# Three small moves in the schedule of an attention and GLU kernel: a late weight's buffers, the gates' exponentials and additions, and the routing's steps

## The chip, the cores and the metric

The kernel runs on one core of a Trainium2 chip. The core has five engines that work side by side and meet only at semaphores: TensorE (PE in the profile; PEld is its loading of weights), VectorE (DVE), ScalarE (ACT), GpSimd (POOL) and SyncE (SP), which issues the DMAs. The metric is the device time of one launch in microseconds (us), the median of several runs. Before the change it is 1688.54 us, from three runs of 1688.06 to 1691.13.

## What is computed

One input `x` of 2048 tokens by 512 features goes through two branches, and a gate per token mixes them. All data are float32.

```python
x = A_x
g = _sigmoid((x * gate_w).sum(-1, keepdims=True))     # routing: one number per token
# branch A: attention, 32 heads of 16 features, softmax over all 2048 keys, then wo
scores = jnp.einsum("bhqd,bhkd->bhqk", q, k) * scale
p = _softmax(scores, axis=-1)
o = jnp.einsum("bhqk,bhkd->bhqd", p, v)
a = o.transpose(0, 2, 1, 3).reshape(B, S, D) @ wo
# branch B: gated linear unit with 1792 inner features
h = _sigmoid(x @ w_gate) * (x @ w_up)
b = h @ w_down
return g * a + (1 - g) * b
```

## The kernel before

**Arithmetic.** Most products are made from operands split into a high and a low part (`split`, L99; `terms`, L142): three matmuls, high by high, high by low and low by high, stand for one float32 product. A split is a copy on one engine (high) and a subtraction on another (low), and a matmul that takes the low part waits for both.

**Stages.** First the queries and keys of the first heads, and the values, are made. Then come 256 periods (`for k in range(NPER)`, L889). A period k treats two of the 16 blocks of 128 keys for one pair of heads and one half of the queries (L668): it makes eight tiles of scores, which ACT turns into exponentials (`st_part`, L681), and then the value products (`values`, L821, matmuls of L829), which add up exponentials times values and, in a 17th row, the softmax's denominators. The sums of eight periods are collected by POOL (L846) and stored to `pv_d`. In each period up to k = 244 there also run eight tiles of scores for a later pair, of which DVE takes the maximum (`sm_step`, L292 to L294). When the 64 tiles of a half are done (`count`, L296), which is at k % 8 == 4, DVE makes the half's maxima out of them and transposes them (L298, L300), and POOL splits them. In the gaps of the row groups TensorE computes everything else in `dense` halves (L162): the remaining queries and keys, the gates and ups of the GLU, and the first heads' share of `wo`. A closing stage (from L945) then runs over 28 chunks (`for n, (c, f) in enumerate(chunks)`, L1009): it multiplies pairs of hidden feature blocks with `w_down` (L1019), with the remaining part of `wo` in between (L149), and stores the output.

**What sets the order.** The order on TensorE, ACT, DVE and POOL is that in which the code issues the instructions. Within a period it is written out by hand in a string, one for periods with maxima and one for the last eleven (`FREE` is 245, `NPER` 256):

```python
STEADY = ("m1:3 t0:2 m0:4 d1 d1 t0:5 m0:6 d1 d1 t0:1 d1 m0:3 d1 t0:2 turn m0:0 t1:4 "
          "m1:5 d0 d0 t1:1 t1:6 d0 m1:2 d0 m1:3 d0 t1:4 d0")
LAST = "t0 d1 t0 d1 t0 d1 turn t0 t1 t1 d0 t1 d0 t1 d0"
```

`m` is a tile of maxima, `t` a tile of scores with its exponential, `d` a half of the dense work, and the number a PSUM bank. A bank is free for the next tile when DVE or ACT has read it. POOL's work waits in lists with an estimated cost for each step and is issued in portions (`work`, L182). Only SP's queue, which issues nearly all DMAs in order, is put in order by the framework's planner from its own estimates.

**The places of the change.**
- *Routing.* `logits` (L814) is DVE's product of 128 tokens with `gate_w`, with a sum. The loop calls it for two blocks of tokens in each group of six periods from k = 75 to 122, at r = 3 and r = 4 of the group (L902). The tokens lie in a tile with the tag `ev`, of which there are two buffers.
- *Denominators.* `denominators` (L781) is a generator: a load, reciprocals on DVE (L787), a store. The loop takes one step of the first chain of them after the value products in each of the periods 192 to 211 (L928). What POOL multiplies with the heads later comes from `rec_d`, which it stores.
- *Early hidden chunks.* The first two chunks of the GLU's hidden layer are made inside the last periods (`hidden_early`, L749). Their gates and ups are loaded at k = 239. Their eight exponentials run on ACT, two in each of the periods 242 to 245, ahead of the value products (L919). The rest are 32 small DVE steps: additions of one (`tensor_scalar`, L759), reciprocals (L763), products (L766), and the split into `xh` and `xl` (L770, L772). The loop takes one of them after the value products of k = 243 and 244 and three after those of each later period. From k = 245 on DVE also empties the value products' bank (L836) and the bank of the dense work (through `leave`, an operation listed under L469), which ACT does before.
- *Late weights.* The rows of `w_down` from the third block on are loaded and split late (`down_late`, L723, called by `late_next`, L950, once before the closing stage and once after each chunk). ACT makes the high parts and POOL the low ones. Weights 2 and 3 go to buffers of the tags `wh` and `wl`, weights 4 and 5 to those of `sum` and `part`, which hold the value products' sums and the last addend before that, and the others to tiles of their own. The two buffers of the tag `wr` hold raw weights; the last of these, `wd0r` and `wd1r`, are split by POOL at k = 241 and 242. A raw late weight lies in an `ev` buffer, which comes free when POOL has made the low parts.

Of the kernel before, what the change touches and what calls it, by code (L numbers as in the profile page):

```python
# [37 lines left out]
NPER = NSTEP // 2  # L38
FREE = NPER - LEAD // 2
# [7 lines left out]
def gated_mix(ctx, tc, x, xT, wqk, wv, wo, w_gate, w_up, w_down, gate_w, out):  # L47
# [51 lines left out]
    def split(h, l, src, hi, lo):  # L99
        if hi is act:  # L100
            act.activation(h, src, AF.Copy)  # L101
        else:
            hi.tensor_copy(h, src)
        return lo.tensor_tensor(l, src, h.bitcast(F32), ALU.subtract)  # L104
# [66 lines left out]
    def turn(*runs):  # L171

        token = pool.nop()
        tc.add_manual_dep(token.ins, runs[-1].last.ins.name, SYNC, reason=SHARED)
        for r in runs:
            r.token = token
# [5 lines left out]
    def work(length):  # L182
        length -= over[0]
        while length > 0.3 and (later or turnover or slow):
            cost, step = (later or turnover or slow).pop(0)
            step()
            length -= cost
        over[0] = max(0.0, -length)
# [52 lines left out]
    def load_pair(p, cols=slice(0, S)):  # L241
        for t, src in enumerate((q_d, k_d)):
            for b in range(2):
                rows, r = slice((2 * p + b) * DH, (2 * p + b + 1) * DH), 64 * b
                to = (QS, KS)[t][p % 2]
                if t == 0:
                    two, one = src[:, rows, cols].rearrange("a d s -> d a s"), src[0, rows, cols]
                else:
                    two, one = src[0, rows, cols].unsqueeze(1), src[1, rows, cols]
                    two = two.to_broadcast([DH, 2, cols.stop - cols.start])  # L250
                sp.dma_start(to[r:r + 2 * DH, cols].bitcast(F32), two)
                sp.dma_start(to[r + 2 * DH:r + KM, cols].bitcast(F32), one)
# [50 lines left out]
    def put_max(half):  # L303

        p, i = half
        mt = mrow.pop(half)
        hl = keep.tile([P, 2, 32], F32R, name=f"mhl{p}_{i}", tag="mhl", bufs=2)

        def low():
            pool.tensor_tensor(hl[:, 1, :], mt, hl[:, 0, :].bitcast(F32), ALU.subtract)  # L310
            d = max_d[2 * p + i]
            sp.dma_start(d.rearrange("k r a j -> (k r) a j"), hl.bitcast(F32))
            for b in (1, 0):
                for a in range(2):
                    r = 64 * b + 3 * DH + a
                    rows_in[p, i] = sp.dma_start(QS[p % 2][r:r + 1, i * 1024:(i + 1) * 1024].rearrange(
                        "o (t k j) -> o t k j", t=8, k=4).bitcast(F32),
                        d[:, 8 * b:8 * b + 8, a, :].rearrange("k t j -> t k j").unsqueeze(0))
        return [(1.6, lambda: pool.tensor_copy(hl[:, 0, :], mt)), (0.25, low)]  # L319
# [348 lines left out]
    def st_part(k, b):  # L668

        p, r = divmod(2 * k, 32)  # L670
        i, kt = divmod(r, 16)
        qs, ks = QS[p % 2], KS[p % 2]
        r = 64 * b
        pt = ptile[k, b] = mid(f"p{k}_{b}")
        for a in range(2):
            for c in range(2):
                o = bank()
                q0 = i * 1024 + c * 512
                pe.matmul(o, ks[r:r + KR, (kt + a) * P:(kt + a + 1) * P], qs[r:r + KR, q0:q0 + 512],  # L679
                          start=True, stop=True)  # L680
                act.activation(pt[:, 2 * a + c, :], o, AF.Exp, scale=DH ** -0.5)  # L681
                yield
# [29 lines left out]
    def hidden_load(c, f):  # L712
        gu = big(f"gul{c}_{f}").rearrange("p (a f s) -> p a f s", a=2, f=2)
        for a in range(2):
            sp.dma_start(gu[:, a], gu_d[a, f:f + 2, :, c * 512:(c + 1) * 512].rearrange("f p s -> p f s"))
        return gu

    def late_raw(src, r):
        raw = keep.tile([P, 2, D], F32, name=f"late{r}", tag="ev", bufs=2)
        sp.dma_start(raw, src[r * P:(r + 2) * P, :].rearrange("(k p) d -> p k d", p=P))  # L720
        return raw

    def down_late(f, raw):  # L723
        if f < 6:
            th, tl, bufs = ("wh", "wl", 4) if f < 4 else ("sum", "part", 2)
            for a in range(2):
                h = keep.tile([P, D], F32R, name=f"wd{f + a}h", tag=th, bufs=bufs)
                l = keep.tile([P, D], F32R, name=f"wd{f + a}l", tag=tl, bufs=bufs)
                split(h, l, raw[:, a, :], act, pool)
                wd.append((h, l))  # L730
        else:
            fs = slice(f - 6, f - 4)
            split(wd_h[:, fs, :], wd_l[:, fs, :], raw, act, pool)
            wd.extend((wd_h[:, f - 6 + a, :], wd_l[:, f - 6 + a, :]) for a in range(2))
# [58 lines left out]
    def split_load(r):  # L793
        f, t, c = r // 8, r // 4 % 2, r % 4
        e = split_in[r] = keep.tile([P, 2, 512], F32R, name=f"sq{r}", tag="ev", bufs=2)
        sp.dma_start(e[:, 0, :].bitcast(F32), s_d[t, f, :, c * 512:(c + 1) * 512])

    def split_sum(r):
        f, t, c = r // 8, r // 4 % 2, r % 4
        e = split_in.pop(r)  # L800

        def store():
            for a in range(2):
                sp.dma_start((q_d, k_d)[t][a, (2 + f) * P:(3 + f) * P, c * 512:(c + 1) * 512],
                             e[:, 1 - a, :].bitcast(F32))
        split_later(e[:, 1, :], e[:, 0, :], e[:, 0, :].bitcast(F32), store)
# [3 lines left out]
    def logit_load(t):  # L810
        tok[t] = keep.tile([P, 2, D], F32, name=f"xn{t}", tag="ev", bufs=2)
        sp.dma_start(tok[t], x[t * P:(t + 2) * P, :].rearrange("(t p) d -> p t d", p=P))

    def logits(t, a):  # L814
        xn = tok[t][:, a, :]
        dve.tensor_tensor_reduce(xn, xn, gwb, scale=1.0, scalar=0.0, op0=ALU.mult, op1=ALU.add,
                                 accum_out=logit[:, t + a:t + a + 1])
# [50 lines left out]
    def emit(order, **parts):  # L868

        for word in order.split():  # L870
            if word == "turn":
                if run:
                    turn(run)
                work(2.0)
            else:
                kind, _, b = word.partition(":")
                spot[:] = [seven[int(b)]] if b else []
                next(parts[kind], None)
# [10 lines left out]
    for k in range(NPER):  # L889
        n = 2 * k  # L890
        if n + LEAD == NSTEP:
            bank = bank7
            leave = dve.tensor_copy
        if 75 <= k < 123:
            t, r = divmod(k - 75, 6)
            if r in (0, 3):
                split_load(2 * t + r // 3)
            if r in (1, 4):
                split_sum(2 * t + r // 3)
            if r == 1:  # L900
                logit_load(2 * t)
            if r in (3, 4):  # L902
                logits(2 * t, r - 3)
        if n % 32 == 0 and n // 32 + 1 < NPAIR:
            load_pair(n // 32 + 1)
        parts["t0"], parts["t1"] = st_part(k, 0), st_part(k + 1, 1) if k + 1 < NPER else iter(())
        emit(STEADY if k < FREE else LAST, **parts)
        if run and run.done():
            run = next(fill, None)
        elif run and run.n:  # L910
            turn(run)
        for half in list(mrow):
            later[:0] = put_max(half)
        work(2.6)
        later.extend(soon)
        soon.clear()
        if k == NPER - 1:
            break
        if NPER - 15 < k <= NPER - 11:  # L919
            for _ in range(2):  # L920
                next(next(exps))
        spot[:] = [seven[SUMS]]
        values(k)
        if k == NPER - 17:
            loaded.extend(hidden_load(*chunks[m]) for m in range(2))
            early = [hidden_early(m) for m in range(2)]
            exps = iter([early[0]] * 4 + [early[1]] * 4)
        if 192 <= k < 212:  # L928
            next(dens[0], None)
        if k == NPER - 6:  # L930
            next(dens[1])
        if k == NPER - 2:
            raws = [late_raw(*late[m][:2]) for m in range(2)]
        if k == NPER - 13:
            early = chain(*early)
        if k >= NPER - 13:
            for _ in range(1 if k < FREE else 3):
                next(early, None)

    flush(later)  # L940
# [133 lines left out]
```

## Time and profile before

The profile shows one execution of 1689.49 us. Its instructions span 1687.7 us; the rest lies before the first and after the last. TensorE was granted its full clock (1.000). The table gives the stages of that execution: bounds from the span's start, and busy time of each engine in us.

| stage | from | to | PE | DVE | ACT | POOL |
|---|---|---|---|---|---|---|
| first products, until the value products of k = 1 | 0 | 96.18 | 94.12 | 81.69 | 36.27 | 12.55 |
| periods with maxima, k = 2 to 244 | 96.18 | 1454.46 | 1358.11 | 1216.32 | 1214.78 | 869.17 |
| last periods, k = 245 to 255 | 1454.46 | 1497.06 | 42.44 | 33.23 | 42.60 | 15.43 |
| closing stage | 1497.06 | 1687.70 | 185.34 | 121.04 | 69.10 | 39.41 |

TensorE's matmuls overlap one another, so that its busy share is near 100% everywhere and says little. More telling is how far apart two like places of the schedule lie: the first matmul of the value products of one period and that of the next.

A row of the timeline reads: start in us, duration, engine, line of the kernel, operation, output and inputs by the program's names, shapes, count. What stands in brackets is the idle time of the engine just before and what ended it. A count over one means that rows close together were merged; the duration is then that of the group. A row of stages ("windows") reads: bounds, length, then busy time of PE, PEld, DVE, ACT and POOL with counts, the granted clock, the DMA engines' busy share and GB/s.

### The profile page before, as it was taken

Reading aid. Unit: us, or ns where it says so; the run is one execution under the profiler, and the core shown is the slowest. Engines: PE = TensorE matmul, PEld = TensorE weight load, DVE = VectorE, ACT = ScalarE, POOL = GpSimd, SP = SyncE. Lnnn points to the kernel's source line nnn. Section 1 sums busy time; section 2 is a strip of 40 time slices with the busy share of each in tenths; the row PEclk is TensorE's granted clock in tenths of the full one; section 3 lists DMA queues with packets and bytes.
Section 4 is the critical chain, followed back from the end, with each engine's and each line's share of the span. In section 5 each row is a group of like instructions: output and inputs, shape, how many; then the busy total and the mean of one; then the engine's idle time right before and its main releaser. Section 6 shows DMA issues by size and latency. Waiting matters only on the chain.

```text
span 1687.7 us, 34644 instructions
## 1 busy us (share of the span) xinstructions
PE 1680.0 (100%) x12485; PEld 1026.4 (61%) x12485; DVE 1452.3 (86%) x2347; ACT 1362.8 (81%) x2657; POOL 936.6 (55%) x920
## 2 busy tenths in 40 slices
PE   9999999999999999999999999999999999999999
PEld 7755555555555555555555555555555555558887
DVE  7988888888889999999888888889998888787753
ACT  4188898988988898889898898989888888984331
POOL 1034476647656666566676766666666667543110
PEclk9999999999999999999999999999999999999999
DMA  7511447366555554555635353534343435358862
GB/s 237 148 46 59 127 175 210 133 165 207 149 194 137 163 153 153 162 162 187 158 102 146 102 145 107 139 102 135 102 129 114 133 113 169 106 184 282 299 216 71
DMA packets 143756, 254.20 MB, mean 151 GB/s; under 512 B 24224, under 2 KB 36512, under 8 KB 140704
## 3 DMA queue, kind: packets, MB, share of 16 engines
q1 hardware_dynamic: 135968, 237.30, 46.2%
q10 hardware_dynamic: 7616, 14.68, 2.7%
q8 instruction: 98, 1.61, 0.4%
q14 instruction: 74, 0.61, 0.1%
HBM read 149.42 MB, written 102.50 MB: 149 GB/s over the span
## 4 chain that ended last, share of the span: by engine, by line
PE 97%; issue 1%; DVE 1%; POOL 0%; DMA 0%; ACT 0%; SPq 0%; POOLq 0%; DVEq 0%
PE dn L162 30%; PE sm L829 27%; PE sm L292 13%; PE st L679 7%; PE sm L1019 5%; PE sm L679 4%; PE st L292 2%; PE dn L1019 2%; PE st L162 2%; PE st L1019 2%; PE st L643 1%; PE st L149 1%; PE sm L149 1%; PE st L829 0%; DVE stat L294 0%
## 5 line engine op out<-in xcount | busy, mean ns | idle before, releaser
L294 DVE TENSOR_REDUCE stat<-sm 128x1 f32<-128x512 f32 x1313 | 849.4, 682 | 142.1 <-PE sm L679 129.3
L681 ACT ACTIVATE p<-st 128x512 f32<-128x512 f32 x1019 | 619.4, 655 | 1.1 <-PE st L679 0.6
L681 ACT ACTIVATE p<-sm 128x512 f32<-128x512 f32 x1027 | 611.6, 633 | 0.8 <-PE sm L679 0.5
L292 PE MATMUL sm<-ks,qs 48*128 48x512 f32 x1313 | 516.3, 435 | 0.2
L294 DVE TENSOR_REDUCE stat<-st 128x1 f32<-128x512 f32 x735 | 479.9, 681 | 0.1
L829 PE MATMUL sm<-p,v 128*17 128x512 f32 x4016 | 480.0, 595 | 0.0
L679 PE MATMUL sm<-qs,ks 64*128 64x512 f32 x1027 | 427.3, 419 | 0.0
L679 PE MATMUL st<-qs,ks 64*128 64x512 f32 x1019 | 426.1, 419 | 0.2 <-ACT p L681 0.2
L292 PEld LDWEIGHTS sm<-ks,qs 48*128 48x128 f32 x1313 | 234.0, 184 | 291.7 <-DVE stat L294 211.5
L846 POOL TENSOR_TENSOR sum<-sum,part 128x512 f32<-128x512 f32 x224 | 288.6, 1288 | 136.0 <-PE sm L679 119.0
L292 PE MATMUL st<-ks,qs 48*128 48x512 f32 x735 | 290.4, 395 | 0.0
L829 PEld LDWEIGHTS sm<-p,v 128*17 128x17 f32 x4016 | 93.1, 96 | 225.9 <-issue 155.1
L834 ACT ACTIVATE part<-sm 128x512 f32<-128x512 f32 x214 | 128.1, 599 | 126.5 <-issue 86.0
L542 POOL TENSOR_TENSOR chain<-chain,chain 128x512 f32<-128x512 f32 x96 | 124.0, 1292 | 156.8 <-PE sm L679 143.1
L679 PEld LDWEIGHTS st<-qs,ks 64*128 64x128 f32 x1019 | 187.5, 184 | 29.9 <-issue 3.4
L679 PEld LDWEIGHTS sm<-qs,ks 64*128 64x128 f32 x1027 | 189.4, 185 | 9.9 <-issue 5.1
L542 POOL TENSOR_TENSOR had<-chain,had 128x512 f32<-128x512 f32 x96 | 123.5, 1286 | 40.1 <-PE sm L679 17.1
L292 PEld LDWEIGHTS st<-ks,qs 48*128 48x128 f32 x735 | 137.1, 187 | 1.4 <-ACT v L662 0.3
L607 ACT ACTIVATE chain<-dn 128x512 f32<-128x512 f32 x128 | 89.1, 696 | 0.0
L542 POOL TENSOR_TENSOR side<-side,side 128x512 f32<-128x512 f32 x32 | 41.3, 1291 | 78.6 <-PE sm L679 74.1
L104 POOL TENSOR_TENSOR ol<-ot,oh 128x512 fp32r<-128x512 f32 (+1 forms) x8 | 15.0, 1871 | 98.2 <-ACT oh L101 84.4
L319 POOL CAST mhl<-mt 128x32 fp32r<-128x32 f32 x32 | 7.5, 236 | 104.1 <-DVE mt L300 104.1
(913 smaller groups left out, 3223.7 us busy)
## 6 DMA issues: line engine op xcount, KB each, us to landing
gul<-gu_d SPq DMA_DIRECT2D x56, 512.0 KB
had<-gu_d SPq DMA_DIRECT2D x84, 256.0 KB
gu_d<-had SPq DMA_DIRECT2D x84, 256.0 KB
gu_d<-side SPq DMA_DIRECT2D x56, 256.0 KB
pv_d<-sum SPq DMA_DIRECT2D x32, 256.0 KB
qs<-q_d SPq DMA_DIRECT2D x30, 256.0 KB
ks<-k_d SPq DMA_DIRECT2D x30, 256.0 KB
gu_d<-far SPq DMA_DIRECT2D x28, 256.0 KB
```

The costliest lines, as they stand in the source:

```text
L149: pe.matmul(o, a, b, start=(i == 0), stop=(i == len(ops) - 1))
L162: mm = pe.matmul(self.o, a[rows], b[rows], start=(self.n == 0), stop=(self.n == 2 * len(self.ops) - 1))
L292: pe.matmul(t, qs[r:r + KM, qt * P:(qt + 1) * P], ks[r:r + KM, g * 512:(g + 1) * 512], start=True, stop=True)
L294: dve.tensor_reduce(stat[half][:, b, qt % 8, g:g + 1], t, axis=AX.X, op=ALU.max)
L542: pool.tensor_tensor(to, u, w, ALU.add)
L607: leave = lambda e, o: act.activation(e, o, AF.Copy)
L679: pe.matmul(o, ks[r:r + KR, (kt + a) * P:(kt + a + 1) * P], qs[r:r + KR, q0:q0 + 512], start=True, stop=True)
L681: act.activation(pt[:, 2 * a + c, :], o, AF.Exp, scale=DH ** -0.5)
L829: pe.matmul(o[32 * c:32 * c + VW, :], v[:, 2 * k % 16 + a, h * VW:(h + 1) * VW], pts[c // 2][:, 2 * a + c % 2, :], start=(a == 0), stop=(a ...
L834: act.activation(e, o, AF.Copy)
L846: pool.tensor_tensor(s, s, e, ALU.add)
L1019: pe.matmul(down[t], a, b, start=(f == 0 and m == 0), stop=(f == NF - 2 and m == 5))
```

## The change

Four edits, all in the order of the work or in the choice of buffers; no operation is added or removed.

1. The last of the weights that were put into `sum` and `part`, number 5, goes into the two `wr` buffers, its high part in the one and its low part in the other.
2. The second `logits` of a group moves from r = 4 to r = 5 in the groups that begin at k % 8 == 1, which are those at 81 and 105: it moves from k = 85 to 86 and from 109 to 110.
3. The steps of the first chain of denominators skip the periods with k % 8 == 4 and run to k = 214 instead of 211, the same twenty steps.
4. The exponentials of the early hidden chunks begin at k = 241 instead of 242 and end at 244. The DVE steps behind them begin at k = 242 instead of 243; from 245 on a period takes two of them if k is odd and four if it is even, instead of three.

```diff
         if f < 6:
             th, tl, bufs = ("wh", "wl", 4) if f < 4 else ("sum", "part", 2)
             for a in range(2):
+                if f + a == 5:
+                    th = tl = "wr"
                 h = keep.tile([P, D], F32R, name=f"wd{f + a}h", tag=th, bufs=bufs)
                 l = keep.tile([P, D], F32R, name=f"wd{f + a}l", tag=tl, bufs=bufs)
                 split(h, l, raw[:, a, :], act, pool)
...
-            if r in (3, 4):
-                logits(2 * t, r - 3)
+            if r == 3:
+                logits(2 * t, 0)
+            if r == (5 if (k - r) % 8 == 1 else 4):
+                logits(2 * t, 1)
...
-        if NPER - 15 < k <= NPER - 11:
+        if NPER - 16 < k <= NPER - 12:
             for _ in range(2):
                 next(next(exps))
...
-        if 192 <= k < 212:
+        if 192 <= k < 215 and k % 8 != 4:
             next(dens[0], None)
...
-        if k == NPER - 13:
+        if k == NPER - 14:
             early = chain(*early)
-        if k >= NPER - 13:
-            for _ in range(1 if k < FREE else 3):
+        if k >= NPER - 14:
+            for _ in range(1 if k < FREE else 2 if k % 2 else 4):
                 next(early, None)
```

## The prediction

> **What bounds the kernel now.** I read the page first, then the stretch of each period, then DVE, ACT and POOL where a period is too long.
>
> ```profile
> span 1687.7 us, 34644 instructions
> PE 97%; issue 1%; DVE 1%; POOL 0%; DMA 0%; ACT 0%; SPq 0%; POOLq 0%; DVEq 0%
> ```
>
> The chain that ends last is PE for 97% of the span, so an edit gains only where PE stands still, or where the other engines stretch its order. I cut the span at the first value product (L829) of each period; a window from one such start to the next is one period's length.
>
> ```profile
> 554.31:559.89 5.58, 5.58 (x47) 3.23 (x45) 5.48 (x11) 5.00 (x11) 1.61 (x2) 1.00 0.55 139
> 559.89:565.75 5.86, 5.86 (x46) 3.17 (x45) 5.79 (x13) 5.20 (x11) 3.50 (x5) 1.00 0.41 130
> 694.43:700.31 5.88, 5.88 (x46) 3.11 (x44) 5.81 (x13) 5.22 (x11) 3.50 (x5) 1.00 0.41 133
> 1185.99:1191.70 5.71, 5.71 (x46) 3.12 (x44) 5.57 (x12) 5.13 (x11) 2.90 (x5) 1.00 0.18 63
> 1230.76:1236.82 6.06, 5.95 (x46) 3.12 (x44) 5.86 (x12) 5.21 (x11) 2.94 (x5) 1.00 0.18 60
> 1426.56:1454.46 27.90, 27.90 (x222) 16.17 (x220) 24.70 (x42) 26.18 (x55) 22.11 (x20) 1.00 0.57 193
> 1454.46:1458.29 3.83, 3.83 (x32) 1.75 (x30) 2.42 (x6) 3.83 (x9) 1.37 (x3) 1.00 0.20 73
> 1458.29:1494.08 35.79, 35.63 (x272) 16.25 (x271) 27.83 (x39) 35.79 (x75) 13.32 (x12) 1.00 0.24 78
> ```
>
> The first column after the bounds is the length, then come the busy times of PE, PEld, DVE, ACT and POOL. A period with maxima lasts 5.58 (first row; the sixth is five of them, 27.90). Rows two to five are the periods that end with the value products of k = 85, 109, 197 and 205: too long by 0.28, 0.30, 0.13 and 0.48. All four follow a period in which a half's maxima are completed (k % 8 == 4). A last period takes 3.83 at best, but the nine of the eighth row take 35.79 where nine at 3.83 are 34.47: 1.32 too much, with ACT busy throughout.
>
> **Denominators.** Their reciprocals leave k = 196, 204 and 212; the loop runs three periods longer.
>
> ```profile
> 1233.05 0.54 DVE L787 RECIPROCAL den<-den 32x64 f32<-32x64 f32 x1
> 1233.62 0.69 DVE L294 TENSOR_REDUCE stat<-sm 128x1 f32<-128x512 f32 x1
> ```
>
> An undisturbed period's first reduce starts 2.38 after the value products before it (568.13 below, less 565.75). Here it starts 2.86 after 1230.76, which is 0.48 late, exactly the period's excess: PE needs the bank that this reduce frees. Without the reciprocal it could start in time. The reciprocals at other k cost nothing now: DVE has 0.70 idle there (below), more than 0.54. **Term: 0.13 + 0.48 = 0.61 gained.** Load and store of the denominators stay one call from their reciprocals, in the same order on SP.
>
> **Logits.** The second of two goes from k = 85 to 86 and from 109 to 110.
>
> ```profile
> 562.56 0.68 DVE L294 TENSOR_REDUCE stat<-sm 128x1 f32<-128x512 f32 x1
> ```
>
> ```profile
> 566.15 1.27 DVE L294 TENSOR_REDUCE stat<-sm 128x1 f32<-128x512 f32 x2
> 568.13 0.69 DVE L294 TENSOR_REDUCE stat<-sm 128x1 f32<-128x512 f32 x1 [0.70 <-PE sm L679]
> ```
>
> At k = 85 the reduce starts 2.67 after 559.89, late by 0.29, and the period is 0.28 long. Taking the logit away gains 0.28, and 0.30 at 109. But at k = 86 it must fit between 567.35 and 568.13, and POOL is there:
>
> ```profile
> 567.16 0.73 POOL L448 TENSOR_TENSOR side_9r<-side_9r 128x256 f32<-128x256 f32 x1
> ```
>
> The first logit of all met the same POOL operation:
>
> ```profile
> 521.98 1.28 DVE L816 CUSTOM_DVE_ANT_0 xn<-xn,gwb 128x512 f32<-128x512 f32 x1
> ```
>
> ```profile
> 521.98 0.73 POOL L448 TENSOR_TENSOR side_8r<-side_8r 128x256 f32<-128x256 f32 x1
> ```
>
> It took 1.28 and ended 0.55 after POOL's end: it ran only then. At k = 86, with DVE and POOL both 0.28 earlier, POOL works from 566.88 to 567.61 and the logit asks at 567.07; it ends at 568.16, and the reduce due at 567.85 starts at about 568.1: 0.25 late. The like at k = 110. Bounds of one giveback: 0 (DVE comes first) and 0.30 (all of it). I take 0.25, the row at 521.98 being this very pair. **Term: 0.58 - 0.51 = 0.07 gained.**
>
> **Gates' exponentials and additions.** The exponentials go from k = 242..245 to 241..244; there ACT has 27.90 - 26.18 = 1.72 idle in five periods, of which two carry a pair already: 0.57 in each of the other three, and a pair takes 0.80. As the five are no longer for those two pairs (5 x 5.58), I cost the pair at 241 at nothing; without that cover it costs the 0.23 by which it is too long. It reads loads that SP issues from the end of k = 239 on; no row here gives their landing, and if they are late, ACT and all behind it wait. The first addition now comes at k = 242, behind its last reduces:
>
> ```profile
> 1443.70 1.28 DVE L294 TENSOR_REDUCE stat<-sm 128x1 f32<-128x512 f32 x2
> 1445.68 0.69 DVE L294 TENSOR_REDUCE stat<-sm 128x1 f32<-128x512 f32 x1 [0.70 <-PE sm L679]
> ```
>
> ```profile
> 1444.81 1.29 POOL L136 TENSOR_TENSOR wd1l<-wd1r,wd1h 128x512 fp32r<-128x512 f32 x1
> ```
>
> ```profile
> 1450.47 0.41 DVE L759 TENSOR_SCALAR gul<-gul 128x512 f32<-128x512 f32 x1
> ```
>
> The addition takes 0.41 and the gap is 0.70. But it would ask at about 1444.9, and POOL's subtraction began at 1444.81 and ends at 1446.10. If it must wait as the logit did, it ends near 1446.4 and the reduce due at 1445.68 is 0.65 late, with PE behind it. Bounds: 0 and 0.65; I take **0.65 lost**, since POOL is first by 0.08. [...] No row of this trace shows a 512-wide addition behind a POOL operation.
>
> **The last periods.** Here ACT has no slack, and the pair that leaves k = 245 costs it directly:
>
> ```profile
> 1460.80 0.80 ACT L755 ACTIVATE gul<-gul 128x256 f32<-128x256 f32 x2
> ```
>
> That is 0.61 to 0.80 of the 1.32 too much. Most of the rest is DVE's: every second period it also empties the heads' bank, behind three operations of the gates.
>
> ```profile
> 1479.68 0.68 DVE L469 COPY hp<-dn 128x512 f32<-128x512 f32 x1
> ```
>
> ```profile
> 1480.26 0.50 PE L679 MATMUL st<-qs,ks 64*128 64x512 f32 x1
> 1480.50 0.47 PE L162 MATMUL dn<-wo0h,xh 64*128 64x512 f32 x1
> ```
>
> The copy ends at 1480.36, and PE's dn product starts 0.24 behind the product that it should run beside. Two operations at odd k and four at even k leave the copy its time.
>
> ```profile
> L763 DVE RECIPROCAL gul<-gul 128x128 f32<-128x128 f32 x16 | 13.8, 913 | 0.0
> ```
>
> Two periods then hold at most six of these, two value copies and one heads' copy: 6 x 0.913 + 3 x 0.68 = 7.5 of 7.66. Bounds: 0.5 (only the pair's time, part of it hidden) and 1.32 (all). **Term: 1.1 gained**, nearer the upper end, as the pair and the late copies are both named in the rows.
>
> **The late weight.** wd5 now takes the buffers of wd0r and wd1r, last read by POOL at 1446.10, so its split waits for no store.
>
> ```profile
> 1510.43 0.39 PE L1019 MATMUL dn<-wd4l,hl 128*128 128x512 f32 x1
> 1510.66 0.39 PE L1019 MATMUL dn<-wd4h,hl 128*128 128x512 f32 x1
> 1511.57 0.50 PE L1019 MATMUL dn<-wd5h,hl 128*128 128x512 f32 x1 [0.52 <-ACT wd5h L101]
> 1512.93 0.50 PE L1019 MATMUL dn<-wd5l,hl 128*128 128x512 f32 x1 [0.85 <-POOL wd5l L104]
> 1513.27 0.39 PE L1019 MATMUL dn<-wd5h,hl 128*128 128x512 f32 x1
> ```
>
> ```profile
> 1510.89 0.63 ACT L101 ACTIVATE wd5h<-late 128x512 fp32r<-128x512 f32 x1 [5.05 <-DMA pv_d<-sum]
> ```
>
> From 1510.66 on, three steps take 2.61 instead of 3 x 0.23 (the step before them), 0.69: 1.92 lost. ACT's wait of 5.05 goes entirely: wd5h starts at 1505.84. What is late next?
>
> ```profile
> 1506.21 1.28 POOL L104 TENSOR_TENSOR wd4l<-late,wd4h 128x512 fp32r<-128x512 f32 x1
> 1511.59 1.28 POOL L104 TENSOR_TENSOR wd5l<-late,wd5h 128x512 fp32r<-128x512 f32 x1 [4.11 <-ACT wd5h L101]
> ```
>
> ```profile
> 1506.38 2.19 DVE L747 TENSOR_TENSOR gul<-gul 128x1024 f32<-128x1024 f32 x1 [0.25 <-DMA gul<-gu_d]
> 1508.49 1.21 DVE L104 TENSOR_TENSOR hl<-gul,hl 128x1024 fp32r<-128x1024 f32 x1
> ```
>
> DVE's product already waits for POOL's wd4l (2.19, not 1.21). POOL's wd5l now stands behind it and would run from 1508.5 to 1509.75, as in this pair, where POOL asked first and DVE's low part waited:
>
> ```profile
> 1518.27 2.43 POOL L104 TENSOR_TENSOR wd_l<-late,wd_h 128x1024 fp32r<-128x1024 f32 x1 [0.91 <-ACT wd_h L101]
> ```
>
> ```profile
> 1518.36 3.42 DVE L104 TENSOR_TENSOR hl<-gul,hl 128x1024 fp32r<-128x1024 f32 x1
> ```
>
> The low part of hl then ends near 1510.9, where PE wants it at 1510.66: 0.25 lost. Later, PE already meets a low part just as it ends:
>
> ```profile
> PEld sm L1019 <- DVE hl L104: 0.2, 1, 0.2
> ```
>
> It hangs on loads that SP issues behind the late weights' low parts. These move up by most of the 1.92, not all; I take 0.2 more. Bounds: 0 (the loads do not move) and 1.92. **Term: 1.45 gained**, nearer the upper end, since ACT, which splits the late weights, is free 5 us sooner. SP's order is the planner's; I take it as it is now.
>
> **Sum:** 0.61 + 0.07 - 0.65 + 1.1 + 1.45 = 2.6. The profiled run took 1689.49 (span 1687.7 and 1.8 around it) and becomes 1686.9; the median, 0.95 below it, 1688.54, becomes **1685.9**.
>
> **Rivals.**
> *The covers hold* (30%): the logits and the addition get DVE's port first, and the closing stage keeps more: 0.58 + 0.61 + 1.2 + 1.6 = 4.0, 1684.5. For it: POOL leads by only 0.08 to 0.2. Against: two rows of blocking.
> *The loads are the bound of the closing stage* (16%): PE, 1.92 sooner, waits that much more for the low part of hl. The tail's term is 0, the rest 1.13: 1687.4. For it speaks the wait just shown; against, that the late raws are asked for sooner.
> *DVE becomes the bound of the last periods* (12%): at even k it has four operations and two copies, 4 x 0.913 + 2 x 0.68 = 5.0 in 3.83. If the bank of the value products (seven take turns) is needed before odd k's slack repays this, PE waits 1.2 in each of five periods: 6 lost, 1688.54 - 2.6 + 6 = 1692, slower. It decides from 0.5 a period (2.6 in all). Against: each period's copies stand ahead of its own operations, and the two periods together still fit (7.5 of 7.66).
> That the weight would still wait is excluded: nothing reads the new buffers after 1446.10.
>
> **Numbers.** 0.2% (3.4 us) is about what a measurement can tell from no change. My forecast, 42%, reaches from 1685.0 to 1686.8, nearly all within it (34 points; 8 faster). The covers' rival is faster for 27 of its 30 points, the loads' rival is the same, DVE's slower for 7 of 12. So faster 0.35, same 0.58, slower 0.07. The range takes in the first three: the covers' sum with 0.6 of scatter, 1683.9, to the loads' with 0.3, 1687.7.
>
> **What would show it.** Periods 85, 109, 197 and 205 back at 5.58; 86 and 110 at about 5.83 with a logit over 1 us long; the period that ends with the value products of k = 243 at 6.2 with an addition over 1 us; nine last periods near 34.7; no ACT wait for pv_d, and wd4 to wd5 without a gap. I am wrong if these additions and logits stay at 0.41 and 0.68, if a low part of hl stops PE for over 1 us behind 1511, or if DVE's copies run late at odd k.

## The result, and the profile after

The changed kernel takes 1692.5 us, the median of 14 runs (1690.93 to 1694.6), against 1688.56 for the kernel before (14 runs, 1687.62 to 1691.13). The ratio is 1.0022 with a 95% interval of 1.0014 to 1.0030: slower by 3.9 us, where I had forecast 2.6 less. The profiled execution took 1693.09, with a span of 1691.3. Its chain of work that ended last:

```profile
PE 95%; DVE 2%; DMA 2%; issue 0%; POOL 0%; SPq 0%; ACT 0%; DVEq 0%; POOLq 0%; ACTq 0%
```

PE's share fell from 97% to 95%, and DMA and DVE have 2% each: in some stretch of the chain something other than TensorE now decides. To find where, I cut both spans at two marks of the schedule, the first value product of k = 1 and that of k = 255. The two stretches behind the first mark, before:

```profile
1500.05:1687.70 187.65, 182.35 (x809) 148.78 (x808) 118.52 (x108) 66.13 (x72) 37.87 (x19) 1.00 0.67 222
96.18:1500.05 1403.87, 1403.53 (x11027) 806.50 (x11025) 1252.06 (x2104) 1260.36 (x2520) 886.14 (x884) 1.00 0.47 140
```

and after:

```profile
1500.36:1691.30 190.94, 184.26 (x809) 149.92 (x808) 121.82 (x108) 66.13 (x72) 41.49 (x19) 0.99 0.65 217
95.80:1500.36 1404.56, 1404.01 (x11027) 806.02 (x11025) 1255.72 (x2104) 1260.51 (x2520) 886.07 (x884) 1.00 0.47 140
```

The span grew by 3.6: -0.38 ahead of k = 1, where the code is the same, +0.69 in the periods, and **+3.29 in the closing stage**, where I had promised 1.45 less.

**The periods.** The same stages as in the prediction, after the change; the first two rows answer to k = 85 and 86 (109 and 110 are like them, 5.59 and 5.90), then come 197 and 205, 243 and 244, and the nine last periods in two rows:

```profile
560.07:565.65 5.58, 5.58 (x47) 3.30 (x45) 5.31 (x11) 5.00 (x11) 3.09 (x5) 1.00 0.28 101
565.65:571.54 5.89, 5.89 (x47) 3.12 (x45) 5.89 (x11) 5.20 (x11) 5.35 (x7) 1.00 0.31 92
...
1186.14:1191.71 5.57, 5.57 (x46) 3.24 (x44) 5.30 (x11) 4.99 (x11) 2.82 (x5) 1.00 0.18 63
1230.77:1236.35 5.58, 5.58 (x47) 3.24 (x45) 5.31 (x11) 5.01 (x11) 2.87 (x5) 1.00 0.18 64
1442.89:1449.07 6.18, 5.94 (x47) 3.11 (x45) 6.18 (x10) 5.78 (x13) 4.45 (x5) 1.00 0.25 94
1449.07:1455.38 6.31, 6.04 (x46) 3.18 (x44) 6.31 (x10) 5.69 (x13) 3.97 (x4) 1.00 0.11 43
1459.22:1463.05 3.83, 3.83 (x31) 1.78 (x31) 1.76 (x3) 3.83 (x9) 1.22 (x2) 1.00 0.02 2
1463.05:1494.34 31.29, 31.29 (x241) 13.60 (x240) 26.41 (x37) 31.29 (x65) 12.21 (x11) 1.00 0.26 88
```

All four long periods are back at 5.58, and 86 and 110 take over 5.89 and 5.90. Both periods that received an addition are long: 6.18, as foreseen, and 6.31, which I did not foresee. The last nine take 3.83 + 31.29 = 35.12, not 34.7. One period, the one that ends at k = 72, is 0.54 longer than before. In seven of the eight further profiles below it is within 0.08 of its old length, and 0.19 over it in one, so I count it as scatter.

DVE and POOL around the two additions (start, duration), first DVE:

```profile
1444.47 1.48 DVE L761 TENSOR_SCALAR gul<-gul 128x512 f32<-128x512 f32 x1
...
1450.67 1.52 DVE L761 TENSOR_SCALAR gul<-gul 128x512 f32<-128x512 f32 x1
```

then POOL:

```profile
1444.39 1.29 POOL L136 TENSOR_TENSOR wd1l<-wd1r,wd1h 128x512 fp32r<-128x512 f32 x1
...
1450.61 1.29 POOL L136 TENSOR_TENSOR xl<-of,xh 128x512 fp32r<-128x512 f32 x1
```

POOL began 0.08 and 0.06 sooner, and each addition, 0.41 in the row of the prediction, ended only 0.27 and 0.29 after POOL had ended.

**The closing stage.** The stall of 1.92 at wd5 is gone: PE goes from wd4 to wd5 in steps of 0.23. Some ten microseconds later PE stands (PE's timeline, after):

```profile
1510.95 0.39 PE L1023 MATMUL dn<-wd4h,hl 128*128 128x512 f32 x1
1511.18 0.39 PE L1023 MATMUL dn<-wd5h,hl 128*128 128x512 f32 x1
1511.41 0.39 PE L1023 MATMUL dn<-wd5l,hl 128*128 128x512 f32 x1
...
1521.49 0.39 PE L1023 MATMUL dn<-wd_h,hl 128*128 128x512 f32 x1
1523.39 0.50 PE L1023 MATMUL dn<-wd_l,hl 128*128 128x512 f32 x1 [1.51 <-POOL wd_l L104]
1524.48 1.01 PE L1023 MATMUL dn<-wd_h,hl 128*128 128x512 f32 x2 [0.58 <-DVE hl L104]
```

The two stops cost 1.90 - 0.23 = 1.67 and 1.09 - 0.23 = 0.86. Then the granted clock is 0.50 for 3 us (a stage of the same trace):

```profile
1525.00:1528.00 3.00, 3.00 (x9) 2.35 (x8) 3.00 (x2) 0.00 (x0) 2.78 (x1) 0.50 0.93 276
```

Nine steps from 1524.48 to 1528.23 take 3.75 instead of 2.04: 1.71 more. A last stop at 1548.82, where chunk 8 waits for the low part of hl, costs 0.82. Together 5.06, less the 1.92 gained: 3.14 of the 3.29.

Who was late? Following the brackets back, first POOL and ACT, then SP (after):

```profile
1520.13 3.21 POOL L104 TENSOR_TENSOR wd_l<-late,wd_h 128x1024 fp32r<-128x1024 f32 x1 [4.90 <-ACT wd_h L101]
```

```profile
1517.10 1.06 ACT L748 ACTIVATE gul<-gul 128x1024 f32<-128x1024 f32 x1 [5.34 <-DMA gul<-gu_d]
1518.06 1.04 ACT L101 ACTIVATE hl<-gul 128x1024 fp32r<-128x1024 f32 x1
1519.01 1.04 ACT L101 ACTIVATE wd_h<-late 128x1024 fp32r<-128x1024 f32 x1
```

```profile
1511.12 0.37 SPq L720 DMA_DIRECT2D late<-in_w_down_dram  x1
1511.59 0.93 SPq L715 DMA_DIRECT2D gul<-gu_d  x2
```

The same place in SP's queue before the change:

```profile
1506.27 0.33 SPq L848 DMA_DIRECT2D pv_d<-sum  x1
1506.69 0.97 SPq L715 DMA_DIRECT2D gul<-gu_d  x2
1512.90 0.37 SPq L720 DMA_DIRECT2D late<-in_w_down_dram  x1
```

Two entries have changed places. The raw weight of f = 8 (the rows of `w_down` for the blocks 8 and 9, L720) needs the `ev` buffer that comes free when POOL has made wd5's low part, at 1508.83 + 2.27 = 1511.10. Standing first, it holds the load of chunk 5's gates and ups (L715) back until 1511.59, 4.9 us later than before. ACT's rows stand in the order of the code: its sigmoid of chunk 5 waits 5.34 for this load and starts at 1517.10, and only behind it, at 1518.06 and 1519.01, come the high parts of chunk 4's hl and of weight 8, which PE and POOL want.

### The profile page after: what moved, and what is told of

It reads as the page before. It is cut to its first block, busy times and chain, and to the rows that moved or that the text cites. A ratio compares the mean times of both kernels' runs of the same rounds, so it can differ in the third digit from the quotient of the medians.

```text
span 1691.3 us, 34644 instructions
## 1 busy us (share of the span) xinstructions
PE 1682.5 (99%) x12485; PEld 1027.9 (61%) x12485; DVE 1459.3 (86%) x2347; ACT 1363.0 (81%) x2657; POOL 940.1 (56%) x920
## 4 chain that ended last, share of the span: by engine, by line
PE 95%; DVE 2%; DMA 2%; issue 0%; POOL 0%; SPq 0%; ACT 0%; DVEq 0%; POOLq 0%; ACTq 0%
PE dn L162 30%; PE sm L831 27%; PE sm L292 12%; PE st L679 7%; PE sm L679 5%; PE sm L1023 4%; PE st L292 3%; PE st L162 2%; PE dn L1023 2%; DMA gul<-gu_d 1%; PE st L643 1%; PE st L149 1%; PE st L1023 1%; DVE stat L294 1%; PE sm L149 1%; PE st L831 0%
```

## Experiments

**Theory A**: the swap in SP's queue causes the loss. **Theory B**, the rival: the low part of wd5, which POOL now makes beside DVE's low part of hl, slows everything behind it. **Theory C**: the closing stage has gained as I forecast, and the loss is elsewhere. Each experiment lists its median (11 runs; the kernel before, beside them, 1689.0) and its closing stage, mostly as a row like those above, from the value products of k = 255 to the end; the length is the first number behind the bounds. The first 96 us differ by up to 0.87 between profiles of these kernels, though their code there is the same, so the closing stage tells more than the whole span. It scatters too: in the three profiles without edit 1 and with SP's old order, it is 187.65, 187.26 and 187.40 long.

### Edit 1 alone

```diff
+                if f + a == 5:
+                    th = tl = "wr"
```

> Before with edit 1 alone (wd5 into the wr buffers). Theory A (SP's queue: with edit 1 the load of the late raw weight of f=8 stands ahead of the load of chunk 5's gates and ups, which then leave 4.9 us later; the sigmoid of chunk 5 holds ACT, and so the weights of f=8, back): everything up to the closing stage as before, the 1.92 us stall at wd5 gone, then about 2.5 us of waiting at chunk 4, some 8 matmuls at half the clock (1.5) and 0.8 at chunk 8; about +3.3 against before, 1691.9. Theory B (wd5's low part, now between DVE's product and the low part of hl, delays everything behind it by contention of DVE and POOL): the same time, but with SP in the order of before. Theory C (the closing stage is better, as I forecast, and the additions, logits and periods are what went wrong): 1.4 less than before, 1687.1.

Measured: 1691.87 (ratio 1.0016, 1.0008 to 1.0025).

```profile
1499.81:1690.10 190.29, 183.91 (x809) 149.94 (x808) 119.73 (x108) 66.13 (x72) 41.57 (x19) 0.99 0.66 220
```

The closing stage is 2.64 longer than before, with SP's two entries swapped (the raw weight issued at 1510.56, the load at 1511.03). PE stands as in the full change, 1.99 and 0.85 too long at chunk 4, but there is no stop at chunk 8, which I had expected here too. Theory C falls. In the time A and B still agree; the swap is what A names, and B as I had put it expected the old order.

### The other three edits without edit 1

```diff
-                if f + a == 5:
-                    th = tl = "wr"
```

> After without edit 1 (wd5 in sum and part as before; the other three edits stay). Theories A and B: closing stage as before with its 1.92 us stall, and the +0.3 that the traces show by then (denominators -0.6, logits +0.05, additions +1.3, last periods -0.65, k=72 +0.2): 1688.9. Theory C: near after, 1692.

Measured: 1689.59 (ratio 0.9998, 0.9989 to 1.0007).

```profile
1499.54:1686.80 187.26, 182.21 (x809) 148.86 (x808) 118.83 (x108) 65.90 (x72) 39.26 (x19) 1.00 0.67 222
```

SP's order is that of before. The closing stage is 0.39 shorter than before (187.65), most of it at wd5, where the three steps lose 1.59 in this execution and not 1.92. The time cannot be told from before: what I got wrong about the periods nearly cancels what they gained.

### All four edits, with chunk 5 loaded a chunk sooner

```diff
-        if n + 4 < len(chunks):
-            loaded.append(hidden_load(*chunks[n + 4]))
+        for m in {0: (4, 5), 1: ()}.get(n, (n + 4,)):
+            if m < len(chunks):
+                loaded.append(hidden_load(*chunks[m]))
```

> After, with the load of chunk 5 asked for one chunk sooner, so that SP issues it ahead of the late raw weight of f=8; everything else of the change stays, wd5's low part included. Theory A: chunk 5's loads land some 3 to 4 us sooner, the wait at chunk 4 and the half clock behind it go, 4 to 5 us less than after: 1687 to 1688.5. Theory B: the low part of wd5 still runs between DVE's two operations, so 1692 as after.

Measured: 1688.84 (ratio 0.9998, 0.9989 to 1.0006).

```profile
1498.88:1685.80 186.92, 182.34 (x809) 148.71 (x808) 117.05 (x108) 66.50 (x72) 42.21 (x19) 1.00 0.67 222
```

SP's queue in this run:

```profile
1505.55 0.95 SPq L715 DMA_DIRECT2D gul<-gu_d  x2
1509.67 0.37 SPq L720 DMA_DIRECT2D late<-in_w_down_dram  x1
```

With the load ahead of the raw weight, 4.02 of the closing stage come back; the two stops at chunk 4 and the half clock are gone. POOL's low part of wd5 still takes 2.27 here, beside DVE's low part of hl as in the full change. Theory B falls. The median is 0.3 above the range that I had expected, and the stop at chunk 8 stays, 0.79 too long:

```profile
1543.29 0.50 PE L1023 MATMUL sm<-wd2h,hl 128*128 128x512 f32 x1 [0.63 <-DVE hl L104]
```

### Control: before, with the same earlier load

The diff is that of the last experiment, on the kernel before.

> Before with the same move of chunk 5's load (SP's order of the closing stage is that of before). Control: theory A expects no change (within 0.5 of before, 1688.6), since chunk 5 was not late there; if the move itself brings something, it shows here as 1 us or more less.

Measured: 1689.0 (ratio 0.9999, 0.9990 to 1.0008). Its closing stage is 187.40 long (187.65 before). Nothing changes, as expected: SP's order here is that of before, and the earlier request alone brings nothing.

### The swap alone, without any of the edits

`hidden_load` keeps the handle of each DMA (`load`), `late_raw` that of f = 8 (`raw8`), and an edge orders them in SP's queue without a semaphore:

```diff
+            if (c, f) == chunks[5]:
+                tc.add_manual_dep(load.ins, raw8[0].ins.name, BEHIND, reason="behind the raw weights of f = 8")
```

> Before, none of the four edits, but the load of chunk 5 is held behind that of the raw weight of f=8 in SP's queue (an ordering edge, no wait). Theory A (the order alone does it): wd5 still waits 1.92 for the store, its low part ends at 1512.87, and only then does SP pass the raw weight and the load of chunk 5: 6 us later than before, so PE waits at chunks 3 to 5 about as much as after does (2.5, a slow stretch of 1.5, 0.8 later): 1692.5 to 1694. Theory B (wd5's low part between DVE's operations does it): as before, 1689, since wd5 is where it was.

Measured: 1693.21 (ratio 1.0022, 1.0013 to 1.0031).

```profile
1499.78:1692.50 192.72, 183.40 (x809) 148.55 (x808) 115.08 (x108) 66.02 (x72) 38.87 (x19) 1.00 0.66 216
```

The closing stage is 5.07 longer with the new order and none of the edits. The load of the last denominators and those of the first heads' share moved up as well, so it is not the purest swap: 2.76 of the loss is the stop at chunk 4, where the full change loses too, and the later stops, 0.84, 1.18 and 1.21 too long, may come in part from the other loads. Part of the expectation was wrong: wd5 lost not 1.92 but 0.44, since its split started sooner after the store of the sum (see the last section). The load of chunk 5 left at 1511.62, not at 1513.3.

### The additions back to k = 243

On top of the earlier load:

```diff
-        if k == NPER - 14:
+        if k == NPER - 13:
             early = chain(*early)
-        if k >= NPER - 14:
+        if k >= NPER - 13:
```

> The kernel with chunk 5's load asked for sooner (e3), and the DVE steps from k=243 as before, two and four a period still; the exponentials stay a period sooner. Theory P (what the additions cost at 242 and 243 is POOL's operation beside each, which began up to 0.08 us before it): the period that ends at 243 is 5.58 again; the one that ends at 244 too if DVE is first by 0.03 as in before: 1.35 less than e3, 1687.5. If POOL is first there: 0.6 less, 1688.2. Rival (an addition in a period of maxima costs 0.6 wherever it stands, for DVE has no room): the lost 0.6 to 0.7 stays in the periods that end at 244 and 245, 1688.8.

Measured: 1686.8 (ratio 0.9989, 0.9980 to 0.9998), 2.0 less than with the additions at 242 and 243, and 0.7 less than expected. The single runs of the two kernels overlap (1686.07 to 1689.24 and 1687.56 to 1690.92), so the rows say more than the medians. The periods that end at 243 and 244:

```profile
1442.49:1448.07 5.58, 5.58 (x46) 3.23 (x44) 4.88 (x9) 5.58 (x13) 4.38 (x5) 1.00 0.39 146
1448.07:1453.75 5.68, 5.68 (x47) 3.24 (x45) 5.30 (x10) 5.67 (x13) 4.30 (x4) 1.00 0.13 48
```

At k = 243, the same POOL operation stands beside the addition, first DVE, then POOL:

```profile
1449.66 0.42 DVE L761 TENSOR_SCALAR gul<-gul 128x512 f32<-128x512 f32 x1
```

```profile
1449.69 1.53 POOL L136 TENSOR_TENSOR xl<-of,xh 128x512 fp32r<-128x512 f32 x1
```

Here DVE is first by 0.03: the addition takes 0.42, and POOL takes 1.53 instead of 1.29. The kernel before had the same pair there. Its addition began at 1450.47 (the row of 0.41 in the prediction), and POOL 0.03 later:

```profile
1450.50 1.53 POOL L136 TENSOR_TENSOR xl<-of,xh 128x512 fp32r<-128x512 f32 x1
```

The rival, that an addition costs 0.6 in any period with maxima, falls. The two periods give back 1.23. The closing stage is 0.73 shorter as well, and the stop at chunk 8 is not there in this run:

```profile
1498.71:1684.90 186.19, 182.15 (x809) 148.78 (x808) 117.19 (x108) 66.19 (x72) 41.37 (x19) 1.00 0.67 223
```

### Three DVE steps in each last period

On top of the last one:

```diff
-            for _ in range(1 if k < FREE else 2 if k % 2 else 4):
+            for _ in range(1 if k < FREE else 3):
```

> e6 with three DVE steps in each last period as before, instead of two and four. My prediction put about 0.5 us of the last periods down to DVE's late copy of the heads' bank: then this is 0.5 slower than e6, in the eight periods from 246 on. Theory L (those periods go at the pace of ACT's exponentials, 3.91 on average; a period of 3.83 only catches up what the one before it lost): the eight take the same as in e6 to 0.15, with 4.0 and 3.83 in turn instead of 3.92 each.

Measured: 1686.75 (ratio 0.9986, 0.9978 to 0.9995), the same as with two and four. The eight periods behind the value products of k = 246, with two and four:

```profile
1461.42:1492.71 31.29, 31.29 (x241) 13.54 (x240) 25.96 (x37) 31.29 (x65) 12.28 (x11) 1.00 0.28 88
```

and with three, with the last four of them apart:

```profile
1461.34:1492.70 31.36, 31.36 (x241) 14.89 (x240) 26.07 (x37) 31.36 (x65) 12.11 (x11) 1.00 0.26 87
```

```profile
1476.95:1481.05 4.10, 4.10 (x31) 2.06 (x31) 3.98 (x7) 4.10 (x10) 1.29 (x2) 1.00 0.37 77
1481.05:1484.88 3.83, 3.83 (x31) 1.83 (x30) 2.50 (x4) 3.83 (x9) 1.28 (x2) 1.00 0.73 259
1484.87:1488.87 4.00, 4.00 (x32) 2.01 (x31) 3.89 (x6) 4.00 (x10) 1.32 (x2) 1.00 0.23 82
1488.87:1492.70 3.83, 3.83 (x31) 1.80 (x30) 3.02 (x5) 3.83 (x9) 1.27 (x2) 1.00 0.16 58
```

4.10, 3.83, 4.00 and 3.83 add up to 15.76, 3.94 each; over all eight the mean is 3.92, against 3.91 with two and four. A period of 3.83 makes up for the long one before it. ACT is busy throughout all of them, so the mean is its pace, and the spread of DVE's steps bought nothing.

### All later loads a chunk sooner

On top of the additions' experiment, with two and four steps:

```diff
-        for m in {0: (4, 5), 1: ()}.get(n, (n + 4,)):
+        for m in (4, 5) if n == 0 else (n + 5,):
```

> e6 with all later loads of gates and ups asked for one chunk sooner, too. In e3 PE still waits 0.8 at chunk 8 for the low part of hl, whose load landed 0.72 late on DVE. If that load's place in SP's queue is why, 0.8 less than e6: 1686.7. If the buffers or DVE's reciprocal of the denominators ahead of it set it, as e6.

Measured: 1686.63 (ratio 0.9983, 0.9974 to 0.9992). Its closing stage is 185.76 long. The 0.8 at chunk 8 that it was to remove was already absent from its base, so it cannot say why chunk 8 had waited; against the base it is 0.17 less, which is no difference. It has the lowest median of all versions, 0.17% below before by the ratio, with the whole interval below 1, but cannot be told from the two versions above.

## Why the prediction was wrong

**The step that failed** is the term of the late weight, +1.45, in its last sentence: "SP's order is the planner's; I take it as it is now." With edit 1 two entries of that order changed places; that it is the planner's estimates that edit 1 moved is likely, but no run looks into them. The term came to -3.29. Three runs settle that the order is the cause: edit 1 alone brings the swap and the loss, undoing the swap alone takes the loss away, and the swap without edit 1 makes a loss again, though not a pure one.

With the order kept, the closing stage is 187.65 - 186.92 = 0.73 shorter than before, and 187.65 - 186.19 = 1.46 in the run with the additions at 243. The difference is the stop at chunk 8. It stands in two of the six profiles with edit 1, and its cause stays open. So the rest of that working was right or half right in size: the 1.92 did go, the 0.25 at wd5's low part did not come, and of the low parts that came late, for which I had allowed 0.2, the one at chunk 8 costs 0.8 or nothing. One execution of before is also a thin base: the stall at wd5 is 1.92, 1.59 and 1.66 in the three profiles without edit 1 and with SP's old order.

The rival "the loads are the bound of the closing stage" was the nearest: a load did become the bound. But I priced it as a gain of nothing, since I let loads come late only by as much as PE came early. The rival "DVE becomes the bound of the last periods" had named 1692, close to the 1692.5 measured, but that is chance: the last periods became shorter, not longer.

**Denominators**, +0.61: measured 0.14 (197) + 0.48 (205) = 0.62. Right.

**Logits**, +0.07: 0.28 + 0.29 gone at 85 and 109, 0.31 + 0.32 given back at 86 and 110 (5.89 and 5.90 against 5.58): -0.06. The mechanism was the one named: the logit, begun 0.11 behind POOL, took 1.18 instead of 0.68. DVE, then POOL (start, duration), at k = 86:

```profile
567.24 1.18 DVE L818 CUSTOM_DVE_ANT_0 xn<-xn,gwb 128x512 f32<-128x512 f32 x1
```

```profile
567.13 0.73 POOL L448 TENSOR_TENSOR side_9r<-side_9r 128x256 f32<-128x256 f32 x1
```

**Additions**, -0.65: the first cost 0.60, as worked out. I never asked where the *second* would stand; it cost 0.73 (6.31 against 5.58). It stands at k = 243, where an addition had cost nothing before, beside the same POOL operation. Both losses come from the 0.06 to 0.08 us by which POOL was first. The term was an estimate from the logit's row, since before the change no addition stood behind a POOL operation. The rows now show both orders: the addition took 1.48 and 1.52 instead of 0.41 where POOL had begun 0.08 and 0.06 before it, and POOL took 1.53 instead of 1.29 where DVE had begun 0.03 before it. At the start I wrote that the engines meet only at semaphores; these rows show more: DVE does not stand idle ahead of the two additions, the additions themselves are longer, by 1.07 and 1.11. That a port is what they wait for, as the covers' rival has it, no run shows.

**Last periods**, +1.1: measured 35.79 - 35.12 = 0.67. The pair of exponentials accounts for 0.51 of it, the period that ends at 246 (4.34 to 3.83). I had taken 3.83, the shortest period of the trace, for the floor, and so saw 0.8 of waste that was ACT's own pace: the eight periods behind the value products of k = 246 took 1494.08 - 1462.63 = 31.45 before and take 31.29 now. The late copy was real in the rows and cost nothing; the run with three steps shows it.

The sum by measured terms: 0.62 - 0.06 - 1.33 + 0.67 - 3.29 = -3.4, and the medians moved by 3.9; the 0.54 at k = 72 is in none of these terms. With SP's order kept the total would have been 0.6 gained, or 1.4 without the stop at chunk 8, not 2.6. The run with the order kept measured 0.2 less than before, which is no difference.

## What to carry to other kernels

Where a planner orders a DMA queue, a change of buffers or dependences can reorder it: read the order of the new program before pricing anything behind it, and ask for a load early enough that it cannot fall behind an entry that waits for a buffer. Take as the floor of a periodic stage the mean of several periods, not the shortest, which may only make up for the one before. For an instruction moved beside another engine's work, place every instance of it, and where the order hangs on less than 0.1 us, price both orders.

## What the runs showed of the hardware

**Half the clock after two stops.** After PE stood 1.51 and 0.58 us with one matmul between them, the granted clock was 0.50 for about 3 us (with edit 1 alone, after stops of 1.83 and 0.58, it was 0.57 from 1525 to 1528). In the run with the swap alone PE stood longer in one piece, and the clock stayed at 1.00:

```profile
1524.40 0.49 PE L1026 MATMUL dn<-wd_l,hl 128*128 128x512 f32 x1 [2.49 <-POOL wd_l L105]
```

```profile
1525.00:1528.00 3.00, 3.00 (x15) 2.45 (x14) 2.14 (x2) 1.44 (x2) 1.49 (x1) 1.00 0.85 258
```

Neither the longest stop nor the idle time in all decides it here: 1.51 + 0.58 = 2.09 us in two pieces were followed by the half clock, 2.49 in one piece were not. What decides is open. In each profile with the order kept the clock is 1.00 over the closing stage, against 0.99 after the change and with edit 1 alone, so I count the 1.71 us of the half clock to the stops.

**From a store to the work that waits for it: 4.6 us, or 3.1.** Before, wd5's split waited until 1510.89 for the store of the sum issued at 1506.27, with two loads of 512 KB issued right behind it. In the two further profiles with this order it took 4.29 and 4.36. With the swap alone, the store issued at 1506.00 let the split start sooner (ACT's timeline, swap alone), with three loads of 256 KB behind it:

```profile
1509.12 0.63 ACT L102 ACTIVATE wd5h<-late 128x512 fp32r<-128x512 f32 x1 [3.73 <-DMA pv_d<-sum]
```

That is 3.1 us from issue to use instead of 4.3 to 4.6. The stall that edit 1 removes may thus have been partly made by the early load on which the next stage depended. It was seen in passing and not tested by itself.
